# Attention and a squared-ReLU feed-forward on one core: when stores, sums, loads and copies are given out, and to which engine

## Chip, cores and metric

The kernel runs on one core of a Trainium2 chip. The metric is the device time of one execution in microseconds (us). PE is the matmul engine (TensorE), with PEld its weight loads; DVE is VectorE, ACT is ScalarE, POOL is GpSimd, SP is SyncE, which here only starts DMAs.

## What is computed

```python
def reference(q, k, v, w_in, w_out):       # q (8, 16, 384, 64); k, v (8, 4, 384, 64); float32
    k, v = repeat(k, 4, axis=1), repeat(v, 4, axis=1)
    attn = softmax(q @ k.T / 8) @ v         # 8 batches, 16 heads
    x = attn.transpose(0, 2, 1, 3).reshape(3072, 1024)
    h = maximum(x @ w_in, 0)                # w_in (1024, 2048)
    return (h * h) @ w_out                  # w_out (2048, 1024)
```

## The kernel before

**Blocks.** A block is one batch: 384 tokens, three tiles of 128. For each block PE computes scores (L437), ACT the exponentials (L447), PE the product with v (L504), DVE divides by the sum (L519), and a DMA on SP transposes the result into xT (L524). Then come the first product, x by w_in (L884), relu (L770 on ACT, L773 on POOL), the square (L778 on ACT, L782 on POOL or DVE), and the second product, h² by w_out (L924, or L1250 in the plain form), whose results are evicted into y_sb (L1055, L1056, L1062) and stored (`store`, L1268). While PE works on the products of one block, the scores and attention of the next one are laid between them.

**Seven products for eight.** From block SB = 2 on the first product uses Strassen's scheme: seven products of half size, on sums of quarters of x (`sums`, L633, four on DVE at L642) and of w_in. Each product's result sits in a PSUM bank. `evict` (L846) empties it: three of the seven products are copied to SBUF (L860 on ACT, L863 on DVE, the "kept copies"), others are added to a kept one (L868 on DVE), one goes straight through (L855). From block FAST = 3 on the second product is done in this manner too (`pair_of`, L1015): pair "A" are the block's first two tiles; the tile that is left over waits in `h2x` (copied at L1158 on POOL in blocks 3 and 5) and forms pair "D" with that of the next block, so that blocks 4 and 6 are double, with fourteen products. The operands of these products are the "first sums" (`sum_ops`, L1109, all issued at L1138): four sums n = 0 to 3 in each of two halves of the rows ("part" 0 and 1), each 128x512 in f16. Part 0 is done on POOL, part 1 on DVE. w_out is scaled in pieces for the same purpose (`with_beta`, L1192, on DVE or ACT; sums of pieces at L1207). A large y sum is done on POOL (L1091).

**Ranges.** The f16 blocks need the greatest absolute value of x and v. DVE finds it by reductions (`widest`, L1430; L1419 for v), puts it in `top_w` (L659), two small matmuls spread it over the partitions (`top_spread`, L669) and DVE reads it back (L673).

**What sets the order.** The whole program is first recorded (`Recorder`, L9): `add` notes an operation with the engine, what it reads and writes, and a cost in us; the recorder keeps a clock for each engine, and `when` tells at what time by these costs a value will be there. `emit` (L86) then writes one program per engine, in the order of recording, with semaphore waits. So the planner's costs do not run on the chip; they decide only the order and the engine. The two main loops (L1650 and L1798) choose at each step what PE does next, among candidates with a planned time; `upkeep` (L1577) is called at each step and gives out what the other engines do: loads (`load_pieces`, POOL's queue: k at L263 and L291, q at L298), chores of the next block (duplicating k, L327; v with a column of ones, `aug_v`, L333; transposes on SP), squares, first sums (`d_q`), x sums (`next_sum`, `add_sums`), widest values, tops, and pieces of w2 (`w2_q`). A store is put on SP's queue at L1287 as soon as its eviction is recorded (`put`), so that SP, which works in order, stops there until the value is there. Most waits of a POOL or SP instruction hold up whatever is behind it in the same queue.

Of the kernel before, what the change touches and what calls it, by code (L numbers as in the profile page):

```python
# [141 lines left out]
def bass_gqa_attention__then__ffn_squared_relu_kernel(  # L142
# [609 lines left out]
    def close_squares(which):  # L752

        for x in [x for x in open_squares if which(x)]:
            open_squares.remove(x)
            i, r, dst, keys, relu, b = x
            val = hr[r]
            two = val.rearrange("p (f t) -> p f t", f=2)
            end = R.ops[i]["end"]
            act, dve, pool = [max(R.clock[e], end) for e in ("scalar", "vector", "gpsimd")]  # L760
            slack = 1.5 * (b >= FAST and keys[0][1:] not in LAST_SQUARES)
            plans = [(act + 0.45 * (1 + relu) + slack, "ss"), (max(act + 0.52 * relu, pool) + 0.77 + 0.2, "sg")]
            if relu:
                plans.append((pool + 2.2 + 0.6, "gg"))
            elif not ff["now"]:
                plans.append((dve + 0.95 + 0.4, "sv"))
            one, other = min(plans)[1]
            to, by = small(b)
            if relu and one == "s":
                R.add("scalar", lambda e, val=val, to=to: e.activation(val, val, AF.Relu, scale=to),  # L770
                      reads=[("hr", r)] + by, writes=[("hr", r)], cost=0.45)
            elif relu:
                R.add("gpsimd", lambda e, val=val, to=to: e.tensor_scalar(val, val, to, 0.0, ALU.mult, ALU.max),  # L773
                      reads=[("hr", r)] + by, writes=[("hr", r)], cost=1.42)
            for _, c, t in keys:
                wrote[c, t] = b
            if other == "s":
                R.add("scalar", lambda e, dst=dst, two=two: e.activation(dst, two, AF.Square),  # L778
                      reads=[("hr", r)], writes=keys, cost=0.45)
            else:  # L780
                eng = dict(g="gpsimd", v="vector")[other]
                n = R.add(eng, lambda e, dst=dst, two=two: e.tensor_tensor(dst, two, two, ALU.mult),  # L782
                          reads=[("hr", r)], writes=keys, cost=0.77 if other == "g" else 0.95)
                if other == "v":
                    hr_read[r] = (n,)
# [39 lines left out]
    def strassen(b, carried):  # L825
# [20 lines left out]
        def evict(prod, j, at):  # L846
            src = bank(at)[:, 0:S]
            if prod in KEPT or prod == 4:
                waiting = [x[1] for x in open_squares]
                r = min((r for r in range(NHR - 2) if r not in kept.values()),  # L850
                        key=lambda r: (r in waiting, R.when(writes=[("hr", r)], eng="vector")))
                close_squares(lambda x: x[1] == r)
                if prod == 4:
                    to, by = small(b)
                    R.add("vector", lambda e: e.tensor_scalar(hr[r][:, :], src, to, 0.0, ALU.mult, ALU.max),  # L855
                          reads=[("bank", at)] + by, writes=[("hr", r)], cost=0.48, after=hr_read.pop(r, ()))
                else:
                    kept[prod, j] = r
                    if R.clock["scalar"] + 0.3 < R.clock["vector"]:
                        R.add("scalar", lambda e: e.copy(hr[r][:, :], src),  # L860
                              reads=[("bank", at)], writes=[("hr", r)], cost=0.45, after=hr_read.pop(r, ()))
                    else:
                        R.add("vector", lambda e: e.tensor_copy(hr[r][:, :], src),  # L863
                              reads=[("bank", at)], writes=[("hr", r)], cost=0.48, after=hr_read.pop(r, ()))
                    return
            else:
                r = kept.pop((ADDED[prod], j))
                R.add("vector", lambda e: e.tensor_tensor(hr[r][:, :], src, hr[r][:, :], ALU.add),  # L868
                      reads=[("bank", at), ("hr", r)], writes=[("hr", r)], cost=0.49, after=hr_read.pop(r, ()))
# [145 lines left out]
    def pair_of(b, pair, one, two):  # L1015
# [53 lines left out]
        def done(prod, at):  # L1069
# [14 lines left out]
            elif prod == 7:  # L1084
                if g1 == g2:
                    slot("a3")
                else:
# [1 line left out]
                added(at, g2, "a2", "a3")  # L1089
                y, z = ys["a3"], ys["p5"]  # L1090
                R.add("gpsimd", lambda e: e.tensor_tensor(y_sb[z], y_sb[z], y_sb[y], ALU.add),  # L1091
                      reads=[("y", y), ("y", z)], writes=[("y", z)], cost=1.1)
                put(two, 1, "p5")
            elif prod == 3:
                added(at, g1, "b2", "b2")
# [13 lines left out]
    def sum_ops(b, double):  # L1109
# [14 lines left out]
        def op(pair, n, part):  # L1124
# [3 lines left out]
            k21, k22 = [("h2T", k, t) for k in ks for t in t2], [("h2T", 8 + k, t) for k in ks for t in t2]  # L1128
            k11, k12 = ([("h2T", k, 0) for k in ks], [("h2T", 8 + k, 0) for k in ks]) if pair == "A" else ([("h2x", b - 1)],) * 2
            key = lambda n: [("DS", b, pair, n, x) for x in parts]  # L1130
            reads = (k21 + k22, key(0) + k11, k12 + key(1), k21 + k11)[n]
            over = [("xT", b % NXT, NKC // 2 * x + i) for x in parts for i in range(NKC // 2)] if pair == "A" else [("DS", b, "A", n, x) for x in parts]

            def go():
# [1 line left out]
                out, p, q, how = ((s1, a21, a22, ALU.add), (s2, s1, a11, ALU.subtract), (s4, a12, s2, ALU.subtract),  # L1136
                                  (a21, a21, a11, ALU.subtract))[n]
                R.add("gpsimd" if part == 0 else "vector", lambda e: e.tensor_tensor(out, p, q, how), reads=reads,  # L1138
                      writes=key(n) + (over if n < 3 else []), cost=1.1 if part == 0 else 0.4 if part else 0.72)

            return reads, go

        def all_wrote(cs, ts=(0, 1)):
            return all(wrote.get((c, t)) == b for c in cs for t in ts)

        for part in range(2):
            cs = [x + 4 * part + i for x in (0, 8) for i in range(4)]
            for n in (0, 1, 3, 2):
                reads, go = op("A", n, part)
                d_q.append((lambda part=part, cs=cs: (("low", "high")[part], b) in flags and all_wrote(cs), reads, go, False))  # L1150
        if double:
            for n, prod in ((0, 5), (1, 6), (3, None), (2, 3)):
                reads, go = op("D", n, None)
# [36 lines left out]

    def with_beta(eng, dst, src, reads, writes, after=()):
        R.add(eng, lambda e: e.activation(dst, src, AF.Copy, scale=o_beta) if eng == "scalar" else e.tensor_scalar(dst, src, o_beta, None, ALU.mult),  # L1192
              reads=reads + ["o_beta"], writes=writes, cost=0.95 if eng == "scalar" else 0.42, after=after)

    def scaled2(n, q, z, eng="vector"):
        with_beta(eng, t_out[n][:, 2 * z:2 * z + 2, :], w2_piece(q, z, w_out_sb), [("w_out",) + QS[q]], [("T2", n, z)] + T_OVER[n])
# [66 lines left out]

    def y_slot(b):
        y_n[0] += 1 + (b >= LEAN and y_n[0] % NY == NY - 1)
        return (y_n[0] - 1) % NY

    def store(b, i3, c0, c1, i):  # L1268
        n = c1 - c0
# [14 lines left out]
    def send(b, i3, c0, c1, yb):  # L1284
# [2 lines left out]
        put = lambda: R.add("sync", lambda e: e.dma_start(rows[:, c0:c1], ysl),  # L1287
                            reads=[("y", yb)], writes=[("out", b, i3, c0)], dma=f"y{yb}", cost=0.6)
        stored.append(("out", b, i3, c0))
        if b:  # L1290
            put()
        else:
            held_back.append(put)

    stored, held_back = [], []

    stretch = [False]

# [90 lines left out]

    def prepare(b):  # L1390

        chores.append(([("k_st", at(b))], lambda: dup_k(b)))
        paced = b > SB + 1

        def go(turn, *args):
            turn(b, *args, gate=tuple(pe_last) if paced else ())
# [11 lines left out]
        for half in range(2):  # L1408
            if b >= LATE and half:
                break  # L1410
            chores.append(([("q_st", at(b), 2 * half, 0)], lambda half=half: go(turn_q_dma, half), paced))
        chores.append(([v_home(b)[1]], lambda: aug_v(b, "gpsimd")))
        halves[:] = [b] if b >= LATE else []
        second.append((go, b, paced))
        values = ("v_st", at(b)) if b < LATE else ("v_aug", b % 2)
# [161 lines left out]
    def upkeep(now):  # L1577
        nonlocal loaded, queued, turned
        pe_last[0:1] = [len(R.ops) - 1 - next(i for i, o in enumerate(reversed(R.ops)) if o["eng"] == "tensor")]
        if loaded + 1 < B and turned >= loaded and not turn_q and not load_pieces and not chores:  # L1580
# [14 lines left out]
                load_q(n, 8, 16)  # L1595
                load_v(n)
            else:
                load_pieces.append(([("k_st", 0)], lambda g: load_k(n, after, g)))
                load_pieces.extend(([("q_st", 0, h // 4, x) for x in range(2)], lambda g, h=h: load_q(n, h, h + 4, after=g))
                                   for h in range(0, H, 4))  # L1600
                if n < LATE:
                    load_pieces.append(([("v_st", 0)], lambda g: load_v(n, g)))
        if load_pieces and now >= dma_at[0] and R.when(writes=load_pieces[0][0], eng="none") <= now:
            load_pieces.pop(0)[1](tuple(pe_last[0:1]))
            dma_at[0] = now + LOAD_GAP
        if not chores and halves and (halves[0] - 1, NU - 1, 5) in scored:
# [2 lines left out]
            queued += 1  # L1609
            prepare(queued)  # L1610
        stretch[0] = split and ff["b"] < SB or bool(ff["now"])
        while chores and R.when(reads=chores[0][0], eng="none") <= now + margin and not (len(chores[0]) > 2 and chores[0][2] and now < dma_at[0]):
            chores.pop(0)[1]()
            if not chores and not halves:
                turned = queued
        while turned > 1 and held_back:
            held_back.pop(0)()
        close_squares(lambda x: not ff["now"] or R.ops[x[0]]["end"] <= now + 0.2)
        while d_q and d_q[0][0]() and R.when(reads=d_q[0][1], eng="none") <= now + 0.3:
            d_q.pop(0)[2]()  # L1620
# [15 lines left out]
        while w_q and w_q[0][0]() and R.when(reads=w_q[0][1], eng="none") <= now and R.clock["vector"] <= now + (0.5 if not ff["tiles"] and not ff["now"] else 0.1):  # L1636
            w_q.pop(0)[2]()
        b = next_sum()
        if b and R.when(reads=[("xT", b % NXT, c) for c in range(NKC)], eng="none") <= now + 0.3:
            add_sums(b)  # L1640
        while w2_q and w2_q[0][0]() and R.when(reads=w2_q[0][1], eng="none") <= now:
            eng = w2_q[0][3]
            lead = {"scalar": 0.1, "vector": -9 if m_q or lazy else 1.0 if below() else 0.5 if ff["b"] == FAST else 0.1}
            able = [x for x in ("vector", "scalar") if eng in (x, "any") and R.clock[x] <= now + lead[x]]
            if not able:
                break
# [3 lines left out]
    while ff["b"] < SB:  # L1650
# [23 lines left out]
        if spread_q and (not split or ff["b"] == 1):  # L1674
            pair = min((p for p in PAIRS if not held & set(p)), key=lambda p: max(open_bank([i]) for i in p), default=None)
            if pair:
                cand.append((max([R.when(reads=["top_w"])] + [open_bank([i]) for i in pair]) + wait, -1 if split else 1.9, "top"))
        at_edge = not ff["now"] and not lanes and not av_open
        if sc_q:
            b, u = sc_q[0]  # L1680
# [117 lines left out]
    while ff["now"] or ff["tiles"] or ff["down"]:  # L1798
# [26 lines left out]
        if spread_q:  # L1825
            pair = min((p for p in PAIRS if not held & set(p)), key=lambda p: max(open_bank([i]) for i in p), default=None)
            if pair:
                cand.append((max([R.when(reads=["top_w"])] + [open_bank([i]) for i in pair]), 2, "top", True))
        if sc_q:
            b, u = sc_q[0]  # L1830
            pieces = later[u]
# [46 lines left out]
            scored |= tiles  # L1878
        else:
            ff_take(bool(ff["tiles"]))  # L1880
    R.add("sync", lambda e: e.nop(), reads=stored)
    R.emit()

# [27 lines left out]
```

## Time and profile before

| | before |
|---|---|
| times of the runs shown | 410.08, 410.44, 412.13 us; median 410.44 |
| the profiled execution | 407.09 us, span 405.3 us |
| PE busy | 393.6 us (97%), 6784 matmuls |
| DVE busy | 319.3 us (79%), 659 instructions |
| ACT busy | 256.1 us (63%), 352 |
| POOL busy | 155.6 us (38%), 177 |
| kept copies | 20 on ACT (0.479 us each), 52 on DVE (0.554) |
| first sums 128x512 | 20 on POOL (1.16), 20 on DVE (0.42 where nothing else holds them) |
| granted PE clock | 1.00 |

The span is the time from the first to the last instruction on the core; the profiled run's own time is 1.79 us longer. A row of waits gives the engine and line that waited, what released it, the total in us, how often, and the longest. In the timeline a bracket at the end of a row gives how long the engine stood idle ahead of it, and the releaser. Matmul ends are modelled, so that starts are the safer measure.

### The profile page before, as it was taken

The numbers are of one execution on the slowest core, as the hardware profiler recorded it, in microseconds if no ns is written. First come the engines' busy times: TensorE is split into PE (matmuls) and PEld (weight loads), VectorE is DVE, ScalarE is ACT, GpSimd is POOL, SyncE is SP. The second block draws the span as 40 slices with busy tenths as digits, with TensorE's granted clock in tenths as the row PEclk, the third lists the DMA queues.
The fourth block names the chain that finished last, engine by engine and source line by source line (L and its number), as shares of the span: only waits on it lengthen the run. The fifth ranks groups of instructions, "written<-read, shape, count | busy, mean of one in ns | idle before, by whom it ended". The sixth has DMA issues, their size and how long they took to land. (4 is left out here: it accounts for less than half of the span.)

```text
span 405.3 us, 15128 instructions
## 1 busy us (share of the span) xinstructions
PE 393.6 (97%) x6784; PEld 278.1 (69%) x6784; DVE 319.3 (79%) x659; ACT 256.1 (63%) x352; POOL 155.6 (38%) x177
## 2 busy tenths in 40 slices
PE   8998999999998999999997999999999999999997
PEld 6565764455645995569863997449974998559944
DVE  3688779843977889999989888877889887847745
ACT  6947960079894889689885679525885586114610
POOL 8665410166410432034573355312561254114710
PEclk9999999999999999999999999999999999999999
DMA  9999999894984051699368918883160312112003
GB/s 171 176 198 188 206 189 174 117 263 56 176 117 158 3 87 36 140 153 182 36 87 115 168 38 107 105 180 102 23 101 28 100 23 42 65 67 81 3 27 129
DMA packets 97201, 44.76 MB, mean 110 GB/s; under 512 B 77552, under 2 KB 91120, under 8 KB 97136
## 3 DMA queue, kind: packets, MB, share of 16 engines
q0 software_dynamic: 36672, 17.44, 34.4%
q1 hardware_dynamic: 59792, 25.86, 29.1%
q8 instruction: 53, 0.87, 0.9%
q10 hardware_dynamic: 672, 0.49, 0.4%
q14 instruction: 12, 0.10, 0.1%
HBM read 35.65 MB, written 12.58 MB: 119 GB/s over the span
## 5 line engine op out<-in xcount | busy, mean ns | idle before, releaser
L447 ACT ACTIVATE expT<-ps 128x1024 bf16<-128x1024 f32 (+1 forms) x118 | 115.0, 1016 | 24.5 <-PE ps L437 24.1
L924 PE MATMUL ps<-w_out_sb,h2T 64*128 64x512 f16 (+1 forms) x464 | 84.0, 376 | 1.2 <-DVE y_sb L1062 0.8
L884 PE MATMUL ps<-xT,w_in_sb 64*128 64x192 f16 x1152 | 84.3, 243 | 0.4 <-DVE y_sb L1062 0.3
L884 PEld LDWEIGHTS ps<-xT,w_in_sb 64*128 64x128 f16 x1152 | 70.9, 94 | 3.0 <-DVE y_sb L1062 0.5
L782 POOL TENSOR_TENSOR h2T<-hr 128x384 f16<-128x384 f32 (+1 forms) x50 | 40.8, 838 | 45.6 <-ACT hr L770 45.2
L884 PE MATMUL ps<-s_all,wx 64*128 64x192 f16 x768 | 52.0, 243 | 0.5 <-DVE hr L868 0.5
L437 PE MATMUL ps<-qT,kT 64*128 64x256 bf16 (+2 forms) x336 | 50.0, 325 | 0.6 <-ACT expT L447 0.6
L1250 PE MATMUL ps<-w_out_sb,h2T 128*128 128x512 bf16 (+3 forms) x240 | 49.5, 365 | 0.0
L868 DVE TENSOR_TENSOR hr<-ps,hr 128x384 f32<-128x384 f32 x72 | 39.4, 555 | 8.3 <-PE ps L884 5.9
L884 PEld LDWEIGHTS ps<-s_all,wx 64*128 64x128 f16 x768 | 44.2, 94 | 2.3 <-DVE hr L868 1.0
L924 PEld LDWEIGHTS ps<-w_out_sb,h2T 64*128 64x128 f16 (+1 forms) x464 | 32.4, 94 | 19.1 <-DVE y_sb L1062 1.3
L600 PE MATMUL ps<-xT,w_in_sb 64*128 64x384 bf16 x448 | 43.0, 323 | 1.8 <-DMA w_in_sb<-in_moe_w_in_dram 1.4
L924 PE MATMUL ps<-area,xT 64*128 64x512 f16 x224 | 43.3, 376 | 1.0 <-DVE y_sb L1056 1.0
L770 ACT ACTIVATE hr<-hr,bits 128x384 f32<-128x384 f32 x60 | 35.7, 608 | 10.2 <-DVE hr L868 9.6
L1250 PEld LDWEIGHTS ps<-w_out_sb,h2T 128*128 128x128 bf16 (+1 forms) x240 | 22.3, 98 | 25.1 <-issue 0.8
L504 PE MATMUL ps<-v_aug,expT 64*128 64x65 bf16 x1440 | 36.8, 190 | 0.1
L504 PEld LDWEIGHTS ps<-v_aug,expT 64*128 64x128 bf16 x1440 | 33.3, 94 | 2.2 <-PE ps L504 0.2
L863 DVE COPY hr<-ps 128x384 f32<-128x384 f32 x52 | 28.3, 554 | 6.6 <-PE ps L884 4.8
L600 PEld LDWEIGHTS ps<-xT,w_in_sb 64*128 64x128 bf16 x448 | 22.2, 94 | 16.4 <-DVE bits L696 1.7
L884 PE MATMUL ps<-xT,wx 64*128 64x192 f16 x384 | 32.3, 243 | 0.1
L884 PE MATMUL ps<-s_all,w_in_sb 64*128 64x192 f16 x384 | 32.2, 243 | 0.0
L860 ACT COPY hr<-ps 128x384 f32<-128x384 f32 x20 | 9.6, 479 | 30.6 <-PE ps L884 30.6
(148 smaller groups left out, 751.7 us busy)
## 6 DMA issues: line engine op xcount, KB each, us to landing
out_dram<-y_sb SPq DMA_DIRECT2D x44, 256.0 KB, 2.5
w_in_sb<-in_moe_w_in_dram POOLq DMA_DIRECT2D x8, 512.0 KB, 15.6
w_out_sb<-in_moe_w_out_dram POOLq DMA_DIRECT2D x4, 1024.0 KB, 29.4
q_st<-in_q_dram POOLq DMA_DIRECT2D x19, 192.0 KB, 4.5
q_st<-in_q_dram POOLq DMA_DIRECT2D x4, 384.0 KB, 23.9
k_st<-in_k_dram POOLq DMA_DIRECT2D x6, 192.0 KB, 5.8
wx<-in_q_dram POOLq DMA_DIRECT2D x2, 384.0 KB, 8.8
out_dram<-area SPq DMA_DIRECT2D x3, 256.0 KB, 4.8
```

Source lines behind the costliest of these rows:

```text
L437: mm = pe.matmul(ps[:, base + x, m * wide:(m + 1) * wide], kT[at(b)][64 * x:64 * x + 64, u, :], q_cols(b, u // NJ, x, c0, c0 + wide))
L447: R.add("scalar", lambda e: e.activation(dst, src, AF.Exp, scale=0.125), reads=keys, writes=[("expT", slot(b, u), t) for u, _, _ in pieces ...
L504: m = pe.matmul(ps[:, p[x], n * DP:n * DP + D + 1], w, v_aug[b % 2][r, g * NJ + j, 0:D + 1], start=(n + j + y == 0), stop=(n + j + y == 2 ...
L600: m = pe.matmul(bank(4 + xs[x])[:, 0:S], w_in_sb[r, kc, c * 128:(c + 1) * 128], xT[b % NXT][r, kc, :], start=(phase < 2 and kc == 0), stop ...
L770: R.add("scalar", lambda e, val=val, to=to: e.activation(val, val, AF.Relu, scale=to), reads=[("hr", r)] + by, writes=[("hr", r)], cost=0.45)
L782: n = R.add(eng, lambda e, dst=dst, two=two: e.tensor_tensor(dst, two, two, ALU.mult), reads=[("hr", r)], writes=keys, cost=0.77 if other ...
L860: R.add("scalar", lambda e: e.copy(hr[r][:, :], src), reads=[("bank", at)], writes=[("hr", r)], cost=0.45, after=hr_read.pop(r, ()))
L863: R.add("vector", lambda e: e.tensor_copy(hr[r][:, :], src), reads=[("bank", at)], writes=[("hr", r)], cost=0.48, after=hr_read.pop(r, ()))
L868: R.add("vector", lambda e: e.tensor_tensor(hr[r][:, :], src, hr[r][:, :], ALU.add), reads=[("bank", at), ("hr", r)], writes=[("hr", r)], ...
L884: return lambda pe: pe.matmul(bank(at)[:, f * h:f * h + h], w[r, kc, c:c + 128], m[r, kc, :], start=(prod in (1, 5, 2) and y + f + kc == 0 ...
L924: return lambda pe: pe.matmul(bank(p.at)[:, 0:512], p.a(k, r), p.w(k, r), start=start, stop=stop, skip_group_check=True)
L1250: m = pe.matmul(bank(i)[:, 0:n], h2[:, c, i3 * 128:(i3 + 1) * 128], w2[:, c, c0:c1], start=(c == 0), stop=(c == NFC - 1))
```

## The change

The change has seven parts. What runs on PE is the same set of matmuls.

1. Planner costs follow other values (relu with a scale, POOL's y sum, first sums, scaled pieces of w2).
2. A kept copy goes to ACT when the planner's ACT clock less 0.1 is under DVE's; before, ACT's clock had to be 0.3 under it. This holds from block FAST on.
3. First sums: before, POOL did all four sums of part 0 and DVE all four of part 1. After, POOL does n = 0 and 1 of part 0, DVE n = 0 and 1 of part 1, and then n = 3 and n = 2 for both parts at once, 128x1024. n = 3 overwrites what n = 0 read, and so waits for it.
4. Stores from block FAST on are kept in `puts` and put on SP's queue when by the planner's clock the value is there, or when the buffer is wanted again, or at the end.
5. The duplicating of k and `aug_v` are given out 2.0 us after their data's landing by the plan (blocks over 3); a load 2.0 us after its buffer is free; the x sums of blocks from FAST on 3.3 us after the transposes' landing.
6. Pieces of w2 may go to DVE in block FAST when its clock is up to 0.5 ahead of PE's, whether or not tops or x sums are outstanding.
7. The top spread is a candidate for PE 0.8 us after `top_w` by the plan.

```diff
-                      reads=[("hr", r)] + by, writes=[("hr", r)], cost=0.45)
+                      reads=[("hr", r)] + by, writes=[("hr", r)], cost=0.54 if by else 0.45)
...
-                    if R.clock["scalar"] + 0.3 < R.clock["vector"]:
+                    if R.clock["scalar"] + (0.3 if b < FAST else -0.1) < R.clock["vector"]:
...
-                      reads=[("y", y), ("y", z)], writes=[("y", z)], cost=1.1)
+                      reads=[("y", y), ("y", z)], writes=[("y", z)], cost=1.28)
...
-            reads = (k21 + k22, key(0) + k11, k12 + key(1), k21 + k11)[n]
+            reads = (k21 + k22, key(0) + k11, k12 + key(1), k21 + k11 + key(0))[n]
...
-                      writes=key(n) + (over if n < 3 else []), cost=1.1 if part == 0 else 0.4 if part else 0.72)
+                      writes=key(n) + (over if n < 3 else []), cost=1.13 if part == 0 else 0.4 if part else 0.62)
...
-        for part in range(2):
-            cs = [x + 4 * part + i for x in (0, 8) for i in range(4)]
-            for n in (0, 1, 3, 2):
-                reads, go = op("A", n, part)
-                d_q.append((lambda part=part, cs=cs: (("low", "high")[part], b) in flags and all_wrote(cs), reads, go, False))
+        for part, n in ((0, 0), (0, 1), (1, 0), (1, 1), (None, 3), (None, 2)):
+            cs = [x + 4 * y + i for x in (0, 8) for i in range(4) for y in range(2) if part in (y, None)]
+            reads, go = op("A", n, part)
+            d_q.append((lambda part=part, cs=cs: ("low" if part == 0 else "high", b) in flags and all_wrote(cs), reads, go, False))
...
     def y_slot(b):
...
-        return (y_n[0] - 1) % NY
+        y = (y_n[0] - 1) % NY
+        put_away(lambda z: z == y)
+        return y
...
-        if b:
+        if b >= FAST:
+            puts.append((yb, put))
+        elif b:
             put()
...
+    def put_away(which):
+        for x in [x for x in puts if which(x[0])]:
+            puts.remove(x)
+            x[1]()
...
-        chores.append(([v_home(b)[1]], lambda: aug_v(b, "gpsimd")))
+        chores.append(([v_home(b)[1]], lambda: aug_v(b, "gpsimd"), False, 2.0 * paced))
...
-                load_pieces.append(([("k_st", 0)], lambda g: load_k(n, after, g)))
+                load_pieces.append(([("k_st", 0)], lambda g: load_k(n, after, g), after))
...
-        if load_pieces and now >= dma_at[0] and R.when(writes=load_pieces[0][0], eng="none") <= now:
+        if load_pieces and now >= dma_at[0] and R.when(writes=load_pieces[0][0], reads=(load_pieces[0] + ((),))[2], eng="none") + 2.0 <= now:
...
+        put_away(lambda y: R.when(reads=[("y", y)], eng="none") <= now)
...
-        if b and R.when(reads=[("xT", b % NXT, c) for c in range(NKC)], eng="none") <= now + 0.3:
+        if b and R.when(reads=[("xT", b % NXT, c) for c in range(NKC)], eng="none") + 3.3 * (b >= FAST) <= now + 0.3:
...
-            lead = {"scalar": 0.1, "vector": -9 if m_q or lazy else 1.0 if below() else 0.5 if ff["b"] == FAST else 0.1}
+            lead = {"scalar": 0.1, "vector": 0.5 if ff["b"] == FAST else -9 if m_q or lazy else 1.0 if below() else 0.1}
...
-                cand.append((max([R.when(reads=["top_w"])] + [open_bank([i]) for i in pair]) + wait, -1 if split else 1.9, "top"))
+                cand.append((max([R.when(reads=["top_w"]) + 0.8] + [open_bank([i]) for i in pair]) + wait, -1 if split else 1.9, "top"))
```

More of the change, by code (lines that the diff above doesn't have):

```diff
@@ L1192, in with_beta @@
         R.add(eng, lambda e: e.activation(dst, src, AF.Copy, scale=o_beta) if eng == "scalar" else e.tensor_scalar(dst, src, o_beta, None, ALU.mult),
-              reads=reads + ["o_beta"], writes=writes, cost=0.95 if eng == "scalar" else 0.42, after=after)
+              reads=reads + ["o_beta"], writes=writes, cost=1.07 if eng == "scalar" else 0.42 if after == () else 0.54, after=after)
     def scaled2(n, q, z, eng="vector"):
@@ L1293, in send @@
             held_back.append(put)
-    stored, held_back = [], []
+    stored, held_back, puts = [], [], []
+    def put_away(which):
+        for x in [x for x in puts if which(x[0])]:
+            puts.remove(x)
+            x[1]()
     stretch = [False]
@@ L1390, in prepare @@
     def prepare(b):
-        chores.append(([("k_st", at(b))], lambda: dup_k(b)))
         paced = b > SB + 1
+        chores.append(([("k_st", at(b))], lambda: dup_k(b), False, 2.0 * paced))
         def go(turn, *args):
@@ L1611, in upkeep @@
         stretch[0] = split and ff["b"] < SB or bool(ff["now"])
-        while chores and R.when(reads=chores[0][0], eng="none") <= now + margin and not (len(chores[0]) > 2 and chores[0][2] and now < dma_at[0]):
+        while chores and R.when(reads=chores[0][0], eng="none") + (chores[0] + (False, 0.0))[3 if len(chores[0]) > 3 else -1] <= now + margin and not (len(chores[0]) > 2 and chores[0][2] and now < dma_at[0]):
             chores.pop(0)[1]()
@@ L1827, in bass_gqa_attention__then__ffn_squared_relu_kernel @@
             if pair:
-                cand.append((max([R.when(reads=["top_w"])] + [open_bank([i]) for i in pair]), 2, "top", True))
+                cand.append((max([R.when(reads=["top_w"]) + 0.8] + [open_bank([i]) for i in pair]), 2, "top", True))
         if sc_q:
@@ L1880, in bass_gqa_attention__then__ffn_squared_relu_kernel @@
             ff_take(bool(ff["tiles"]))
+    put_away(lambda y: True)
     R.add("sync", lambda e: e.nop(), reads=stored)
```

## The prediction, made before the changed kernel ran

> **What bounds the kernel now.** I read the page first, then PE's waits, then windows and timelines around the waits found. Engine rows and chain of the page:
>
> ```profile
> PE 393.6 (97%) x6784; PEld 278.1 (69%) x6784; DVE 319.3 (79%) x659; ACT 256.1 (63%) x352; POOL 155.6 (38%) x177
> ...
> PE 42%; DVE 2%; ACT 1%; issue 0%
> ```
>
> TensorE (PE) is busy for 393.6 of 405.3 us, and the change leaves its 6784 matmuls as they are. So only the 11.7 us in which PE is not busy can be won. PE's waits name the releasers:
>
> ```profile
> PE ps L669 <- DVE top_w L659: 2.8, 2, 1.6
> PE ps L600 <- DMA w_in_sb<-in_moe_w_in_dram: 1.4, 1, 1.4
> PE ps L924 <- DVE y_sb L1056: 1.0, 1, 1.0
> PE ps L924 <- DVE y_sb L1062: 0.8, 1, 0.8
> ```
>
> (total us, times, longest.) Except for the one weight load at 36 us, the releasers are VectorE (DVE). The windows from 190 us on (PE, PEld, DVE, ACT, POOL busy) show it full just there:
>
> ```profile
> 190.00:200.00 10.00, 9.47 (x269) 8.66 (x266) 9.90 (x22) 9.17 (x15) 6.03 (x8) 1.00 0.28 53
> 200.00:210.00 10.00, 9.73 (x205) 7.34 (x199) 8.84 (x20) 7.81 (x13) 6.08 (x6) 1.00 0.68 94
> 210.00:220.00 10.00, 9.22 (x92) 4.35 (x87) 9.97 (x17) 7.86 (x8) 4.80 (x5) 1.00 0.97 119
> ```
>
> The granted clock is 1.00. The largest stall, in the timeline:
>
> ```profile
> 219.95 0.38 PE L924 MATMUL ps<-w_out_sb,xT 64*128 64x512 f16 x1
> 220.33 1.00 DVE L1430 TENSOR_REDUCE bits<-o_sb 128x1 f32<-128x384 f16 x2
> ...
> 221.89 0.20 PE L669 MATMUL ps<-ident,top_w 64*128 64x64 bf16 x2 [1.57 <-DVE top_w L659]
> ```
>
> These matmuls start every 0.21 us (219.73, 219.95), so the lost time is 221.89 − 219.95 − 0.21 = 1.73, which is 0.16 over the bracket. I count every stall so (bracket plus 0.16): **A** 123.6 us, spread L669 after block 1, 1.42; **B** five between 196.4 and 207.3 (0.68, 0.18, 0.23, 0.25, 0.30), 1.64, mostly DVE L868; **C** 213.4, DVE L1062, 0.95; **D** 220, above, 1.73; **E** 304.9, DVE L1056, 1.17; **F** 364, block 6 to 7, 0.67; **G** 270.7, 0.12. Together 7.70 us: more than that this change can't win by the trace, 1.9% of the time.
>
> **The change part by part.** Placements come from the two instruction streams side by side, durations from the trace of before.
>
> *Top spread (+0.8).* The planner takes the widest value as later by 0.8, so the spread goes one piece of four matmuls later at A: 4 x 0.21 = 0.86 us of work that now stands behind the wait goes ahead of it. A falls from 1.42 to 0.56: gain **0.86** (0 to 1.42).
>
> *Kept copies (L859) and w2 pieces.*
>
> ```profile
> L863 DVE COPY hr<-ps 128x384 f32<-128x384 f32 x52 | 28.3, 554 | 6.6 <-PE ps L884 4.8
> L860 ACT COPY hr<-ps 128x384 f32<-128x384 f32 x20 | 9.6, 479 | 30.6 <-PE ps L884 30.6
> ```
>
> Nine copies go from DVE (43 stay) to ScalarE (29): DVE loses 9 x 0.554 = 5.0 us, ScalarE gains 9 x 0.479 = 4.3. The pieces of w2 (L1192: DVE 0.48 to 1.05, ScalarE 1.14) are no longer kept from DVE in block 3 while a top or x sum is due, and so are given out sooner: the last of them is out some 120 matmuls earlier, ahead of the stretch that is full. That is the gain's reason. DVE's timeline shows them as B's backlog: two L1192 pieces, 1.90 us from 194.74, stand right ahead of the L868 that starts at 196.56 and that PE waits for, and L1207's sums of such pieces (0.68 to 0.90) and L863 copies (0.55) stand ahead of the next ones. Without the pieces 1.64 falls to some 0.4: gain **1.2** (0.3 to 1.6). It has a price: near 180 us ScalarE now has five pieces (5 x 1.14 = 5.7 us) ahead of a kept copy that frees a bank of the next product. By the order some 0.9 of it is not covered by PE's matmuls if all five run back to back; I take half, a new stall of **−0.4** (0 to −0.9).
>
> *First sums.* POOL loses ten sums of 1.16 (L1138), DVE's ten of 0.42 (128x512) become 128x1024, for which the same line's D sums have 0.68: DVE +10 x 0.26 = 2.6 us over five blocks, 0.5 in each. In blocks 3 and 5, POOL's copy of the tile left over (L1158) runs beside them:
>
> ```profile
> 210.76 2.45 DVE L1138 TENSOR_TENSOR xT<-h2T,xT 128x512 f16<-128x512 f16 x1
> 211.02 1.90 POOL L1158 COPY area<-h2T 128x2048 f16<-128x2048 f16 x1
> ```
>
> That sum takes 2.45 for 0.42. C waits behind it. After the change POOL is free some 2.3 us sooner (two sums), the copy starts sooner and meets an earlier sum, and the bank behind that is late by about as much: gain **0** (−0.3 to 0.95). For E:
>
> ```profile
> 302.37 2.14 POOL L1158 COPY area<-h2T 128x2048 f16<-128x2048 f16 x1 [1.16 <-ACT h2T L778]
> 302.80 1.99 DVE L1138 TENSOR_TENSOR xT<-xT,h2T 128x512 f16<-128x512 f16 x1
> ...
> 305.39 0.74 DVE L1056 TENSOR_SCALAR y_sb<-ps,bits 128x512 f32<-128x512 f32 x1
> ...
> 306.18 0.39 PE L924 MATMUL ps<-area,xT 64*128 64x512 f16 x1 [1.00 <-DVE y_sb L1056]
> ```
>
> The bank that PE wants is copied out at 305.39, behind the stretched sum. In the new stream this copy stands ahead of the sum: gain **1.17** (0 to 1.17). Cover of the 0.5 elsewhere: in the double blocks 4 and 6 PE has fourteen products of second-product work and waits for no sum; without that cover it is 2 x 0.5 = 1.0.
>
> The Trainium skill (SBUF — State Buffer, Who interferes with whom) says that a VectorE instruction with two SBUF inputs contends with a GpSimd instruction that reads SBUF, and that the second to issue blocks until the first is done. The trace agrees on the block (the sums end 0.29 and 0.28 us behind the copies), though at 210.76 the sum's record starts ahead of the copy's and it is still the one held. By the rule the sums given to VectorE are exposed to whatever POOL does; that is the first rival.
>
> *D.* DVE's queue from 214.5 to 221.84 is full; in the new stream one reduction of 0.54 (L1430) has gone ahead and first products of the block follow with less behind them: gain **0.6** (−0.3, if the wider sums push it, to 1.73).
>
> *Chores, loads, x sums held 2.0 to 3.3 us.* No PE wait after 81 us ends on a DMA. The x sums (L642) end at 217.1, 261.4, 308.8 and 347.6; PE first reads them at 225.9, 277.4, 317.8 and 366.4: 8.8 us or more of cover, against 3.3. **0**; bare, 2.0 to 3.3 at each of four handovers. A gain from it (DVE turns to a nearer task first) is in D's bounds.
>
> *Stores queued when the value is there.* The SP queue waits 51.0 us at L1287 for DVE L1062 and 43.8 for POOL L1091, with transposes for the next block behind it; those end in x sums (8.8 us of cover) and in score inputs, for which PE waits nowhere after 81 us. The last stores keep their place. **0** (−0.5 to 0.5: the size of one DVE turn). G goes: **0.12**. F has the same order around it: **0**.
>
> Sum: 0.86 + 1.2 − 0.4 + 0 + 1.17 + 0.6 + 0.12 = **3.55 us**. The profiled execution took 407.09 (span 405.3 and 1.79 around it), 3.35 below the median of the runs shown, 410.44. The stalls are absolute, so I take them from both: 403.5 for the profiled execution, 410.44 − 3.55 = **406.9** for the median.
>
> **The rivals.**
>
> 1. *POOL's copy catches the wide sums in blocks 3 and 5.* A held 128x1024 sum costs what the held small ones do: 2.45 − 0.42 = 2.03 and 1.99 − 0.43 = 1.56. E's gain is lost and C is 0.3 worse: 410.44 − (3.55 − 1.17 − 0.3) = 408.4. For it: both copies in before hit a sum. Against: in block 5 the copy out of the bank now stands ahead.
> 2. *The stalls only move; the change does nothing that PE sees.* DVE is busy 9.97 of 10 us at 210 to 220, and takes 2.6 us back in sums of the 5.0 it loses in copies. Then B and D return at the next bank, and A and E less the new stall remain: 410.44 − (0.86 + 1.17 − 0.4) = 408.8; with A alone, 409.6. Stores and holds, the larger part of the diff, are hidden in either case.
> 3. *Slower: the kept copies wait on ScalarE.* Each of the nine can come behind an exp of 1.02 us (L447) that has just begun, and its bank comes free that much later than DVE would have freed it: at most 9 x 1.02 = 9.2 us, against 3.95 of gains: 410.44 − 3.95 + 9.2 = 415.7. It decides from six of nine on (6 x 1.02 = 6.1, over 3.95 + 2.05). For it: ScalarE is 9.17 busy at 190 to 200. Against: before the 20 copies it has now, ScalarE idled 30.6 us waiting for PE, so they did not queue.
>
> **How the numbers follow.** Forecast 0.52, near 404.4 to 408.3; rival 1 0.15; rival 2 0.20; rival 3 0.13. About 0.5% (2.05 us) is what a measurement of this kernel can tell from no change. Faster by more (below 408.4): the forecast and half of rival 1, 0.59. Within: the other half and nearly all of rival 2, 0.27. Slower: rival 3 and the least of rival 2, 0.14. All favourable ends together would give 7.0 us (403.4), all unfavourable ones −1.2 (411.6); the range is 403.8 to 411.9, which leaves out a twentieth below and most of rival 3 above.
>
> **What would show it.** Right: the waits of PE on top_w fall from 2.8 to about 1.7, the L924 wait on L1056 is gone, the L884 wait on L868 too, DVE has 43 copies at L863. Wrong: a L1138 sum of over 1.5 us with a PE wait right behind it (rival 1); the same total of DVE-released waits at other lines (rival 2); PE waits on ACT L860 or on banks at 178 to 182 and 230 to 300 us (rival 3); PE waits on q, k or xT, which would break the cover of the holds.

## The result, and the profile after

The changed kernel takes 405.00 us (median of 4, 404.80 to 405.09) against 410.44 for the one before: ratio 0.986, interval 0.983 to 0.989. The forecast was 406.9. Its profiled execution took 404.96 (span 403.1), 2.13 less than the profiled one of before. In every execution of the changed kernel the granted clock was 1.000. (The ratios here leave out executions over 1.5% above their kernel's fastest; medians and counts by clock take them all.)

PE's waits of the changed kernel (total, times, longest):

```profile
PE ps L669 <- DVE top_w L659: 2.2, 2, 1.1
PE ps L504 <- issue: 1.3, 1, 1.3
PE ps L924 <- DVE y_sb L1056: 1.0, 1, 1.0
...
PE ps L884 <- DVE y_sb L1062: 0.6, 2, 0.3
...
PE ps L924 <- DVE y_sb L1062: 0.5, 1, 0.5
```

The list looks much like that of before: the top spread still costs 2.2 in two waits (2.8 before), an L1056 wait is there again, at another place, and 1.3 us are new in which PE waited for nothing that the profile names ("issue"). Nothing here is worth 5.4 us. Of the signs that the prediction named, DVE has its 43 copies at L863, no L884 wait on L868 is left and the top spread fell, though to 2.2 and not 1.7; the L1056 wait is gone at its old place only. The sites, counted as in the prediction (bracket plus 0.16), in the two profiled executions:

| site | before | after | gain | forecast |
|---|---|---|---|---|
| A, spread at 122 to 124 us | 1.42 | 1.30 | 0.12 | 0.86 |
| B, first product of block 3, by DVE | 1.64 | 0.85 | 0.79 | 1.2 |
| new stall near 180, by ScalarE | 0 | 0 | 0 | −0.4 |
| C, first bank in block 3 | 0.95 | 1.16 | −0.21 | 0 |
| D, spread at 218 to 220, and behind it | 1.73 | 1.23 + 0.69 | −0.19 | 0.6 |
| E, bank in block 5 | 1.17 | 0 | 1.17 | 1.17 |
| F and G, and 0.12 at 263 | 0.79 | 0.79 | 0 | 0.12 |
| 350 us, not foreseen | 0 | 0.65 | −0.65 | 0 |
| sum | | | 1.03 | 3.55 |

Left out are the weight load's 1.52 at 36 us and 0.40 for a square at 155 us (before only), "issue" stalls of 1.45 and 0.29 at 184 and 230 and waits of 0.69 and 0.49 for a load and a transpose at 10 and 74 us (after only), and smaller ones; c0 to c11 have more and less of the weight load's and the "issue" stalls. C and E went as worked out. POOL's copy (now L1157) starts at 207.12 instead of 211.02, meets an earlier sum, and the bank's eviction stands behind it:

```profile
207.12 1.90 POOL L1157 COPY area<-h2T 128x2048 f16<-128x2048 f16 x1
207.18 2.14 DVE L1138 TENSOR_TENSOR xT<-xT,h2T 128x512 f16<-128x512 f16 x1
...
209.84 0.74 DVE L1056 TENSOR_SCALAR y_sb<-ps,bits 128x512 f32<-128x512 f32 x1
```

In block 5 the eviction stands ahead of the sum, which is hardly held by then (0.92 for 0.42):

```profile
301.91 0.75 DVE L1056 TENSOR_SCALAR y_sb<-ps,bits 128x512 f32<-128x512 f32 x1 [0.44 <-PE ps L924]
302.58 0.92 DVE L1138 TENSOR_TENSOR xT<-xT,h2T 128x512 f16<-128x512 f16 x1
```

At 350 the first rival's mechanism came in by another door: an x sum (0.55 alone) now runs beside POOL's y sum, takes 1.62, and the bank behind it is late. That the hold of the x sums moved it there is read from the order; no run has that hold alone.

```profile
347.92 1.51 POOL L1091 TENSOR_TENSOR y_sb<-y_sb 128x512 f32<-128x512 f32 x1 [11.49 <-DVE y_sb L1062]
...
348.22 1.62 DVE L642 TENSOR_TENSOR s_all<-xT,s_all 128x768 f16<-128x768 f16 x1
...
350.56 0.39 PE L924 MATMUL ps<-w_out_sb,area 64*128 64x512 f16 x1 [0.49 <-DVE y_sb L1062]
```

So the sites of the forecast gave 1.0 us, and behind the start of block 1's second product even that is spent again. From that product's first matmul (105.42 us before, 103.29 after) to the end of the span, before takes 299.85 and the changed kernel 299.82; all of the 2.13 between the two profiled executions lies ahead of it, its largest piece the weight load's 1.52. The other 3.3 of the 5.4 us are in neither trace, since the profiled execution of before was not a usual one.

### The profile page after: what moved, and what is told of

It reads as the page before. It is cut to its first block, busy times and chain, and to the rows that moved or that the text cites. A ratio compares the mean times of both kernels' runs of the same rounds, so it can differ in the third digit from the quotient of the medians.

```text
span 403.1 us, 15107 instructions
## 1 busy us (share of the span) xinstructions
PE 392.0 (97%) x6784; PEld 292.4 (73%) x6784; DVE 313.2 (78%) x646; ACT 261.5 (65%) x365; POOL 145.5 (36%) x167
## 5 line engine op out<-in xcount | busy, mean ns | idle before, releaser
L447 ACT ACTIVATE expT<-ps 128x1024 bf16<-128x1024 f32 (+1 forms) x118 | 115.3, 1012 | 19.7 <-PE ps L437 19.2
L884 PE MATMUL ps<-xT,w_in_sb 64*128 64x192 f16 x1152 | 85.5, 243 | 0.9 <-DVE y_sb L1062 0.6
L924 PE MATMUL ps<-w_out_sb,h2T 64*128 64x512 f16 (+1 forms) x464 | 84.9, 376 | 0.0
L884 PEld LDWEIGHTS ps<-xT,w_in_sb 64*128 64x128 f16 x1152 | 70.7, 94 | 4.9 <-DVE y_sb L1062 1.0
L437 PE MATMUL ps<-qT,kT 64*128 64x256 bf16 (+2 forms) x336 | 52.1, 324 | 0.5 <-DVE qT L408 0.2
L884 PE MATMUL ps<-s_all,wx 64*128 64x192 f16 x768 | 52.2, 242 | 0.0
L868 DVE TENSOR_TENSOR hr<-ps,hr 128x384 f32<-128x384 f32 x72 | 39.7, 555 | 10.3 <-PE ps L884 6.9
L924 PEld LDWEIGHTS ps<-w_out_sb,h2T 64*128 64x128 f16 (+1 forms) x464 | 38.9, 94 | 11.0 <-DVE hr L855 0.4
L884 PEld LDWEIGHTS ps<-s_all,wx 64*128 64x128 f16 x768 | 44.0, 94 | 0.8
L504 PE MATMUL ps<-v_aug,expT 64*128 64x65 bf16 x1440 | 38.2, 190 | 1.6 <-issue 1.3
L504 PEld LDWEIGHTS ps<-v_aug,expT 64*128 64x128 bf16 x1440 | 35.2, 94 | 3.2 <-issue 1.7
L884 PE MATMUL ps<-xT,wx 64*128 64x192 f16 x384 | 33.2, 243 | 0.0
L860 ACT COPY hr<-ps 128x384 f32<-128x384 f32 x29 | 13.8, 477 | 29.9 <-PE ps L884 29.0
L884 PE MATMUL ps<-s_all,w_in_sb 64*128 64x192 f16 x384 | 33.0, 242 | 0.0
L863 DVE COPY hr<-ps 128x384 f32<-128x384 f32 x43 | 23.7, 555 | 8.1 <-PE ps L884 6.1
```

Of the source, the lines that this page charges most:

```text
L437: mm = pe.matmul(ps[:, base + x, m * wide:(m + 1) * wide], kT[at(b)][64 * x:64 * x + 64, u, :], q_cols(b, u // NJ, x, c0, c0 + wide))
L447: R.add("scalar", lambda e: e.activation(dst, src, AF.Exp, scale=0.125), reads=keys, writes=[("expT", slot(b, u), t) for u, _, _ in pieces ...
L504: m = pe.matmul(ps[:, p[x], n * DP:n * DP + D + 1], w, v_aug[b % 2][r, g * NJ + j, 0:D + 1], start=(n + j + y == 0), stop=(n + j + y == 2 ...
L860: R.add("scalar", lambda e: e.copy(hr[r][:, :], src), reads=[("bank", at)], writes=[("hr", r)], cost=0.45, after=hr_read.pop(r, ()))
L863: R.add("vector", lambda e: e.tensor_copy(hr[r][:, :], src), reads=[("bank", at)], writes=[("hr", r)], cost=0.48, after=hr_read.pop(r, ()))
L884: return lambda pe: pe.matmul(bank(at)[:, f * h:f * h + h], w[r, kc, c:c + 128], m[r, kc, :], start=(prod in (1, 5, 2) and y + f + kc == 0 ...
```

## The experiments

Ratios and medians are against the kernel before on the same chip. "Full clock" counts executions at a granted clock of 1.000. "A" is the stall at the spread near 122 us in the profiled execution, counted as above. Of before there are 97 executions: 28 at full clock (405.08 to 411.15, median 407.85), 49 at 0.995 to 0.996 (median 410.82), 20 lower (413.0).

| run | what | median | ratio | full clock | A |
|---|---|---|---|---|---|
| c0 | before again | 410.3 | 0.999 (0.994 to 1.004) | 2 of 10 | 1.23 |
| c1 | stores alone | 410.1 | 0.999 (0.995 to 1.003) | 3 of 10 | 3.55 |
| c2 | all but stores | 405.7 | 0.992 (0.987 to 0.996) | 6 of 6 | 1.66 |
| c3 | first sums alone | 410.6 | 1.002 (0.997 to 1.006) | 3 of 10 | 3.43 |
| c4 | spread alone | 408.9 | 0.994 (0.990 to 0.998) | 7 of 10 | 0 |
| c5 | loads alone | 407.8 | 0.998 (0.994 to 1.002) | 3 of 10 | 2.37 |
| c6 | filler at A | 408.4 | 0.996 (0.992 to 0.999) | 10 of 10 | 0 |
| c7 | all but spread | 413.2 | 1.008 (1.003 to 1.013) | 2 of 10 | 2.28 |
| c8 | before, two pieces ahead | 409.7 | 1.000 (0.996 to 1.003) | 8 of 10 | 0 |
| c9 | changed, two pieces ahead | 405.5 | 0.989 (0.986 to 0.992) | 8 of 8 | 0 |
| c10 | all but loads | 406.9 | 0.995 (0.990 to 1.000) | 8 of 10 | 2.29 |
| c11 | all but copies and w2 | 408.4 | 0.996 (0.992 to 0.999) | 3 of 10 | 1.50 |

Except in c6, c8 and c9, the planner lays everything behind the edit anew, so a run tells of its part and of the new order together.

**First, where the profile of before lacks 3.3 us.** c0 has no edit; c1, c2 and c3 take the change's hunks for the stores (`puts`) or the first sums alone, or leave the former out.

> The kernel before, unchanged, as a second look. Its profiled execution took 407.09 us and its other runs 410.08 to 412.13, so 3.3 us of the 5.4 won are not in the trace that the prediction was read from. If a single loss sits in most executions and was absent from that one, this profile shows it as one PE stall of about 3 us that the first profile lacks (time 410 to 411); if the profiled execution is simply quicker by its own spread, it comes again near 407 with the stalls of 7.7 us that the prediction listed.

> The kernel before with the stores alone queued when their value is there by the plan. The prediction priced this at 0: then 410.4 within 0.5. Rival, that the 3.3 us which the first profile lacks is a late landing of transposes behind blocked stores: 407 to 408.

> The changed kernel with stores put on the queue at once, as before. By the prediction 405.0 within 0.5; by the rival of late transposes 407.5 to 408.5.

> The kernel before with the first sums alone moved (two of POOL's four to VectorE, in whole ones, and their planner costs). The prediction gave the stall at 305 us, 1.17, to this part, and 0 at 213: 409.3. Rival (POOL's copy catches the wider sums in blocks 3 and 5): 410.4 to 411.5, with a sum at L1138 of over 1.5 us and a PE wait behind it.

c0's profiled execution was again a quick one, 405.52, while the median of its ten was 410.3: neither branch of the expectation, but it showed that before has no one time. c1 finds stores worth nothing, as forecast; c2, at 405.7, is 0.2 above its expected range, and its interval overlaps the changed kernel's. The profiles of c1 and c3 show what the first one lacked. c1's execution took 413.74 us at a clock of 0.992, while c3's, 410.54 at 0.996, is of the most frequent kind. c3's windows from 122 us on (PE, PEld, DVE, ACT, POOL busy, then granted clock, DMA share, GB/s):

```profile
122.00:124.00 2.00, 0.54 (x3) 0.04 (x1) 1.20 (x3) 0.00 (x0) 0.00 (x0) 1.00 1.06 364
124.00:126.00 2.00, 0.20 (x3) 0.17 (x4) 1.90 (x8) 0.00 (x0) 0.00 (x0) 1.00 0.49 181
126.00:128.00 2.00, 2.00 (x7) 0.75 (x7) 0.85 (x4) 1.04 (x1) 0.00 (x0) 0.56 0.37 135
128.00:130.00 2.00, 2.00 (x7) 0.70 (x5) 0.88 (x2) 1.05 (x2) 0.00 (x0) 0.59 0.00 0
130.00:132.00 2.00, 2.00 (x28) 1.44 (x27) 1.58 (x4) 1.46 (x3) 0.00 (x0) 1.00 0.02 7
```

PE stands for 3.43 us, and then the granted clock falls to 0.50, by the trace's clock record from 126.2 to 129.6 us: matmuls that start every 0.21 us start every 0.43 until 129.5. "Busy" hides it, since a slow matmul is busy too. Half speed for 3.4 us is 1.7 us lost, which is a clock of 0.996 over some 408 us. Against the trace of before that is 2.01 more of stall and 1.7 of clock, 3.7 us, where 3.3 were looked for. The stall's cause is on DVE, whose first x sum had to wait for the transposes:

```profile
122.77 0.56 DVE L642 TENSOR_TENSOR s_all<-xT 128x768 f16<-128x768 f16 x1 [3.82 <-DMA xT<-area]
```

c1 shows the same (3.55 and 0.50), and a second fall at 192 us behind an "issue" stall. c3's own part, the first sums, came out as its rival had it: 410.6, with a sum of 2.46 at 213.88 and PE's wait of 1.22 behind it. E fell from 1.17 to 0.60 and C rose to 1.22; the 0.30 between them is lost in the spread of its times.

**Second, what shortens the stall, and whether the clock hangs on it.**

> The kernel before with the top spread alone taken 0.8 us later by the plan (one piece of four matmuls, 0.86 us, ahead of it at site A). Theory: in most executions of before the spread at 122 us stalls PE for 3.4 to 3.6 us, the clock then falls to half for some us, and this is the 3.3 us that the first profile lacks; 0.86 us more of work ahead keeps the stall under 2.7 us and the clock at 1.000: median 406.5 to 407.5, and every execution within 1 us of the others. Rival, the stall comes from late transposes that this part does not touch: 409.5 to 410.5, with clocks of 0.996 as before.

> The kernel before with the loads alone given out 2.0 us later. Theory (the spread is the cause): 410.4 within 0.6, clocks of 0.996 in most executions. Rival: later loads leave the transposes before site A more of the DMA engines, they land 2 us sooner, and the stall at A stays at 1.2 to 1.7 us: 406.5 to 407.5 and clock 1.000.

> The kernel before with eight extra matmuls (8 x 0.21 = 1.7 us) whose results are not used, put on PE right ahead of the spread at site A; nothing else moves. They fill 1.7 us of the stall. Theory (a stall of over 3 us lets the clock fall): the longest stall becomes 1.9 us, the clock stays 1.000, the median 406.5 to 407.5, though PE does 1.7 us more work. Rival (the lower clock has another cause): 410.4 to 411, clocks of 0.996 as before.

> The changed kernel with the top spread where it was. Theory: 408 to 410, clocks of 0.996 in many executions, since the stall at 122 us is again up to 3.5 us. Rival (loads): 405.0 to 406.0 with clock 1.000.

c4 and c7 are the hunks of the spread (`when(top_w) + 0.8`) alone and left out, c5 that of `load_pieces` alone. c6 adds to before, in `top_spread`, for the fourth spread:

```diff
+            def fill(pe):
+                for x in range(8):
+                    m = pe.matmul(ps[:, p, 0:512], ident[:, :], w_out_sb[:, 0, 0:512])
+                return m
+            R.add("tensor", fill, reads=["ident", ("w_out", 0, 0)], writes=keys, cost=0.0)
```

c4 lies between its two expectations: 7 of 10 at full clock, but 408.9. Its new order also makes PE wait 1.22 for a bank at 117.6, ahead of A. c6 is the cleanest: with 1.7 us of useless matmuls in the gap, ten of ten executions run at full clock, where 28 of 97 do without, and the median falls by 2.4 us. Most of the lower clock thus follows from PE's standing still at A (c8, with the gap filled by PE's own work, has 8 of 10). But 408.4 is more than the 407.5 expected at most, so the clock is not all.

c5 shows what the loads do there. I measure from the first matmul of block 1's second product (105.42 us in the first profile). Without the hold the first x sum, which waits for the transposes, starts at 16.5 to 16.8 us in five profiles (before, c0, c4, c6, c8) and at 18.8 to 19.7 in three (c1, c3, c10); with the hold at 17.4 to 17.9 in all six (c5, c7, c2, c9, c11, changed). The four loads of q on POOL's queue start at 2.1 to 10.2 without and 3.8 to 11.9 with it, and the last transpose goes out at 13.7 to 16.0 without and at 11.9 to 12.3 with it. So in these profiles the hold trades two modes of landing for one between them. The rival held for the landing, the theory for the clock: 2.37 us of stall is still too much, and 7 of c5's 10 lose clock. The time, 407.8, is nearer the rival's; it is 3.0 under the median of before on this chip, though the interval of the ratio includes 1.

c7 is the largest difference, and beyond what the theory expected (408 to 410): the change without its spread is slower than before. A is 2.28 and the clock falls. In the new order of block 3 PE waits four times for DVE's o_sb between 179 and 186 (0.26 to 0.91 each), and the clock falls again, from 183.2 to 190.0, far from A; so c7 does not price the spread.

**Third, the two parts together, and the rest.**

> The kernel before with PE's two pieces of four matmuls that follow the spread at site A put ahead of it (8 x 0.21 = 1.7 us); every other engine's order is untouched, and nothing is planned anew. Theory: the stall of 1.2 to 3.6 us becomes 0 to 1.9 us, too short for the clock to fall: 406.5 to 407.5, clock 1.000 in all executions. What is then left to 405.0 is the sum of the other sites, about 2 us. Rival, that the clock falls for another reason, or that a later spread is paid for behind it: 409.5 to 411.

> The changed kernel with the two pieces that still follow the spread at site A put ahead of it as well, nothing else moved. Theory: the stall of 1.3 to 1.7 us left there is filled: 403.5 to 404.3. Rival, the later spread delays the pieces of w2 that hang on it, or the time goes into the next wait: 405.0 within 0.4.

> The changed kernel with the loads given out at once, as before. Theory (the spread is the cause): 405.0 to 406.0, clock 1.000. Rival (later loads let the transposes land sooner and so shorten the stall at A): 406.5 to 408, clock 0.996 in some executions, and a stall of over 2 us at 122 us.

> The changed kernel with kept copies and pieces of w2 given out as before, with their planner costs (parts 2 and 6 and the costs of relu and scaled pieces). The prediction gave these 1.2 less 0.4 us at 180 to 207: then 405.6 to 406.0, with DVE-released stalls of about 1.6 us in that stretch and fewer fetch-like stalls at 184. Rival, that they matter no more than the order's chance: 404.5 to 405.4.

c8 and c9 permute the recorded operations just ahead of `emit`, so that no other engine's order moves (their lines are some nine higher):

```diff
+    def ahead(self, at, pieces):
+        ops = self.ops
+        move = [i for i in range(at + 1, len(ops)) if ops[i]["eng"] == "tensor"][:pieces]
+        order = list(range(at)) + move + [i for i in range(at, len(ops)) if i not in move]
+        place = {i: n for n, i in enumerate(order)}
+        self.ops = [dict(ops[i], need={place[d] for d in ops[i]["need"]}) for i in order]
...
+    R.ahead(spreads[3], 2)
     R.emit()
```

c10 and c11 are the changed kernel without the loads' hunk, and without the hunks of kept copies, `w2_q` and the costs at L771 and L1193.

c8 keeps the clock (8 of 10) and still gains nothing at the median: my theory, that A's stall and the clock are the 3.3 us, falls short there. The trace shows where A's own part goes. ScalarE's timeline and PE's wait in c8:

```profile
127.84 1.15 ACT L1203 ACTIVATE area<-w_out_sb,bits 128x1024 f16<-128x1024 bf16 x1 [0.95 <-DVE area L1203]
128.89 2.83 ACT L456 ACTIVATE expT<-ps 128x1024 bf16<-128x1024 f32 x3
```

The scaled pieces of w_out hang on the spread; the exps are queued behind them, and PE, which came 1.7 us sooner, waits 1.15 for an exp at 128.7. In c9 the same wait is 1.48 for 1.30 filled, and the time 405.5 is not under the changed kernel's: the rival was nearer (405.0 within 0.4). A chain from the transposes by top, spread and scaled piece to the exp sets the time there; matmuls put ahead only keep PE going.

c10 (spread without hold) came out as its rival had it: 406.9, a stall of 2.29 with a fall to 0.50 in its profile, which is the slowest of its ten, and 8 of 10 at full clock (404.4 to 410.3). So neither part does it alone.

How the two parts work together can be read from where the first x sum starts and the spread behind it, before and then changed:

```profile
122.18 0.56 DVE L642 TENSOR_TENSOR s_all<-xT 128x768 f16<-128x768 f16 x1 [1.81 <-DMA xT<-area]
125.21 0.20 PE L669 MATMUL ps<-ident,top_w 64*128 64x64 bf16 x2 [1.26 <-DVE top_w L659]
...
120.79 0.56 DVE L642 TENSOR_TENSOR s_all<-xT 128x768 f16<-128x768 f16 x1 [2.56 <-DMA xT<-area]
123.81 0.20 PE L669 MATMUL ps<-ident,top_w 64*128 64x64 bf16 x2 [1.13 <-DVE top_w L659]
```

From the first matmul of block 1's second product the x sum starts at 16.57, 16.76, 18.77 and 18.89 in c0, before, c3 and c1, and A is 1.23, 1.42, 3.43 and 3.55: A follows the landing one for one. With the hold and the spread's 0.86 it is 17.50, 17.71 and 17.86 (changed, c11, c2) and 1.30, 1.50 and 1.66, the same line lowered by 0.86. So in the late mode the hold takes off 0.9 to 1.4 us and the spread 0.86; in the early mode the hold costs 0.7 to 1.3. (c10's x sum is at 19.73, and PE had lost 1.22 to a bank just ahead, as in c4.)

c11 missed both expectations: 408.4. B's stalls by DVE come to 1.87 there (1.64 expected), but the loss is at D. The windows of c11:

```profile
219.00:221.00 2.00, 0.59 (x6) 0.09 (x2) 2.00 (x7) 0.00 (x0) 1.26 (x1) 1.00 1.52 76
221.00:223.00 2.00, 0.98 (x21) 0.98 (x22) 1.56 (x8) 0.00 (x0) 0.47 (x1) 1.00 0.51 164
223.00:225.00 2.00, 2.00 (x70) 2.00 (x67) 1.93 (x6) 0.00 (x0) 0.32 (x1) 0.62 0.53 56
225.00:227.00 2.00, 2.00 (x31) 2.00 (x28) 0.38 (x1) 0.48 (x1) 0.00 (x0) 0.53 1.05 301
```

DVE's queue is longer by an x sum and reductions, the stall at D becomes 2.60, and the clock falls behind it (A, 1.50, left it at 1.00). With copies on ScalarE and w2 given out sooner it is 1.23. No run beat the changed kernel.

## Why the prediction was right, and where it was not

The direction and the range held. That the forecast's 3.55 and the measured 5.44 are near each other is largely luck: the sites of the sum gave 1.03, and a quick execution of before is as quick behind 105 us as the changed kernel. What the change does, as far as the traces show it, is to keep executions from being slower than that, and this is no term of the sum.

- **The base failed.** "The stalls are absolute, so I take them from both" took the 3.35 us between the profiled execution and the median for a constant. It was a loss of its own: in c3, the one execution of the most frequent kind that was traced with A as before, the late landing at A and the clock's fall behind it are 3.7, and the changed kernel has neither. From 410.5 (all of before's executions) to 407.85 (those at full clock) are 2.65; the other 2.85 down to 405.0 are not assigned, and c8, which fills A and gains nothing at the median, says that they are not at A alone.
- **A was mis-sized.** 0.86 of matmuls did go ahead. In these two traces that saves 0.12, since with the hold the first x sum starts 0.74 later (17.50 for 16.76). Where the stall is filled outright, c8 and c9 show that the wait moves on to an exp. The worth of 0.86 is that, with the hold, a stall of up to 3.55 stays under 1.7. The bounds (0 to 1.42) were those of one execution's stall.
- **The holds, priced at 0, were wrong.** "No PE wait after 81 us ends on a DMA" was read from PE's list. The wait on top_w ended on DVE, which had itself idled 1.81 for "DMA xT<-area", a row of the trace of before. One step further back, the cover was gone. The hold on the loads is worth some 1.1 us of A where the landing is late (3.43 to 3.55 in c3 and c1 against 2.28 to 2.37 in c7 and c5) and costs 0.7 where it is early. The holds on chores and x sums were not run by themselves.
- **B** gained 0.79 for 1.2, and ScalarE's pieces cost nothing near 180. **D**: the spread's own stall fell by 0.50 (0.6 forecast), but DVE's L1062 at 220.69 is late behind it, 0.69: the wait moved on. c11 speaks for parts 2 and 6 as what carries D, together with the new order that they bring.
- **C, E and F** went by the steps given, G's 0.12 came again at 263 us, and **stores** were worth nothing (c1, c2). The size of the 350 us loss, 0.65, was in no step, though its mechanism was the first rival's.
- **Rivals:** 1 in part (C, 350); 2 in part (D); 3 nowhere: no PE wait in the changed kernel ends on ScalarE's copies.
- **The ends of the range** leave out a term: 7.0 and −1.2 are summed without the ±0.5 of the stores.

Open: at full clock c6 and c8 still spread from 406.4 to 410.3 where the changed kernel's four executions keep to 0.3 us, and c8's median is no lower than that of before. Without a trace of those executions I can't say which loss it is; the section on the hardware has a candidate. The even landing at A is one reason why the changed kernel keeps so close; whether it is the only one isn't shown.

## What to carry to other kernels

Before pricing stalls from one trace, hold its time against the unprofiled ones: a gap that the trace does not explain is the first thing to find, and a kernel whose granted clock differs by execution has no one time. Follow a wait back past the engine that released it, until something ends on a transfer or on PE itself. A stall near the length at which the clock falls is worth more than its length. To compare two traces, measure from a mark that both share: it parts what the change did from what came ahead of it.

## What was not expected of the hardware

**The clock.** In all profiles PE's stalls of 1.2 to 1.9 us left the granted clock at 1.00 (the longest 1.90, c7 at 227 us), and those of 2.28, 2.29, 2.37, 2.60, 2.89, 3.43 and 3.55 were followed by a clock of 0.50, each time for 3.4 us by the trace's clock record. A row of shorter ones did it too (c7: 0.83 and 0.26 from 179.7 to 182.5 and a third of 0.91 just begun, when the clock fell at 183.2, for 6.8 us). The Trainium skill (TensorE: Matmul & The Clock Gate, HAM oscillation) gives gaps over about 3.4 us as what brings it; here 2.28 were enough, and the measurement decides. Where between 1.90 and 2.28 the limit lies, or whether it hangs on when the stall falls, isn't shown.

**PE standing with no releaser.** "issue" stalls in the middle of L504, near 184 to 190 us: 0 in two profiles of before, 2.89 in c1, 1.82 in c6, 1.45 in the changed kernel. In c1's waits:

```profile
PE ps L504 <- issue: 2.7, 1, 2.7
```

A candidate is PE's own program. Queue q8, of kind "instruction", carries 53 packets of 16 KB in before, and PE's 13,568 matmuls and weight loads are 53 times 256. In the trace's records they come every 3.7 to 5.1 us from 177 to 197 us in before and c0; in c1 one came at 182.84 and the next only at 189.65, PE's last matmul ahead of the stall started at 189.3, and it went on at 192.2. In c6 and the changed kernel the packet just ahead of the stall came 7.7 us behind the last one. Transposes filled the 16 DMA engines in parts of these stretches, but in before they did so too (182 to 185 us) with no stall, so what delayed a packet stays open. The Trainium skill (Runtime: NRT & Kernel Launch, Instruction fetch mechanics) says that programs are streamed in blocks of 16 KiB by DMA and that this is mostly hidden; the packets agree in size. That a late packet is what stopped PE here, and that it is what spreads the executions at full clock, is argued from these times, not shown.
